# Centering ahead of the transposes and scaling by 1/std behind the projections, in the first segment of a fused attention and gMLP kernel

## The chip, the cores and the metric

The kernel runs on one core of a Trainium2 chip. Its time is the device time in microseconds (us) of one execution. A profiled execution also has a span, 1.7 to 1.8 us shorter than its time. Engines: TensorE (PE in the profile; PEld is its weight load), VectorE (DVE), ScalarE (ACT), GpSimd (POOL), SyncE (SP, which issues the DMAs here).

## The reference, cut to what matters

```python
def _layernorm(x, eps=1e-05):
    m = jnp.mean(x, axis=-1, keepdims=True)
    v = jnp.var(x, axis=-1, keepdims=True)
    return (x - m) / jnp.sqrt(v + eps)
# x: 2048 x 1024, handled in 4 segments of 512 rows; 32 heads of 32
# per segment: q, k, v = xn @ wq, xn @ wk, xn @ wv with xn = _layernorm(x),
# causal softmax attention within the segment, plus a memory of earlier segments
h  = x + A(_layernorm(x))        # attention, then @ wo
h2 = h + B(_layernorm(h))        # gMLP: two gelu halves, a 2048 x 2048 mixing, w_out
```

The change uses that a row's 1/std is one factor for that row: it may be applied to V's rows, and to the columns of transposed q and k, after the projections.

## The kernel before

The kernel records each operation on its engine's list, in program order, and derives waits from overlaps of memory cells of 32 bytes. TensorE and VectorE work their lists off in that order in the traces below (after the change, TensorE's ready V matmuls stand 2.69 us behind one that waits, and VectorE idles 1.53 us with statistics behind it whose chunk ScalarE had read from 4.33 us on). So the order of these lines is the order of work. The head of the kernel normalizes four chunks of 128 rows, transposes them on TensorE and projects V, k and q. Matrix products land in PSUM (ps in the traces), which this kernel lays out as eight banks; copying one out is called its eviction here. The gates are the sigmoid weights between attention and memory, the mask set-up spreads them into the table that the memory state is multiplied by, and phi is the function that the memory applies to q and k.

```python
warm(12)                        # dummy 128x512 matmuls
stats_of(0)                     # VectorE mean and variance, GpSimd 1/std
stats_of(1)
ln0 = ln_apply(XCH[0], ks[0])   # VectorE (x - mean) * rstd, bf16
pe_T(XNT[0], 0, ln0, (act, dve))  # 8 transposes, two copies out of PSUM
warm(3)
ln1 = ln_apply(XCH[1], ks[1])
stats_of(2)
pe_T(XNT[0], 1, ln1)
...                             # V quarters of 8 matmuls 128x256 between the chunks
proj_qk(0, 1); proj_qk(0, 0)    # k, then q, first 128 columns
v_quarter(3, 0); v_quarter(3, 1)
phi_exp(0); phi_max(0)
rot["banks"] = [6, 7]           # from here k, q, V and the memory state share two PSUM banks
# then per group of 4 heads: logits, k, pv, logits, state, q, logits, V ...
```

The eviction of q and k was one ScalarE copy from PSUM, in every segment:

```python
act.activation(QK[n % 2][:, which, :], bank(b), ACTF.Copy)
```

The softmax here doesn't subtract the row's maximum and nothing guards it: scores larger than these inputs give would overflow.

Of the kernel before, what the change touches and what calls it, by code (L numbers as in the profile page):

```python
# [5 lines left out]
BF16 = mybir.dt.bfloat16  # L6
F32 = mybir.dt.float32
I32 = mybir.dt.int32
ACTF = mybir.ActivationFunctionType
ALU = mybir.AluOpType  # L10

T = 2048
D = 1024
H = 32
NSEG = 4
L = 512
# [3 lines left out]
NQ = 8  # L20
# [237 lines left out]
def bass_sequential_preLN__memory_aug_infini_attn__mixer_gmlp__prompt_kernel(  # L258
# [17 lines left out]
    pe, act, dve, pool, sp = R.pe, R.act, R.dve, R.pool, R.sp  # L276

    K = 1024
# [4 lines left out]
    def tens(name, shape, dt, off):  # L283
        sz = int(np.prod(shape[1:])) * mybir.dt.size(dt)
        assert off % 32 == 0 and off + sz <= ARENA, (name, off, sz)
        t = nc.alloc_sbuf_tensor_at(name, list(shape), dt, offset=abase + off)
        R.space[t[:].tensor.name] = ("sbuf", off)
        return t
# [13 lines left out]
    cb = Bump(0, 14 * K)  # L302
    IDENT = cb("ident", [128, 128], BF16)
# [11 lines left out]
    MV = [cb("mv%d" % i, [128, 2], F32) for i in range(4)]  # L315
    RS = [cb("rs%d" % i, [128, 2], F32) for i in range(4)]
    RD = cb("rd", [128, 4, 4], F32)
    RDM = cb("rdm", [128, 4, 4], F32)


    HNT = [tens("hnT0", [128, 8, L], BF16, 14 * K), tens("hnT1", [128, 8, L], BF16, 22 * K),
           tens("hnT2", [128, 8, L], BF16, 30 * K), tens("hnT3", [128, 8, L], BF16, 38 * K)]
    XNT = [tens("xnT0", [128, 8, L], BF16, 30 * K), tens("xnT1", [128, 8, L], BF16, 38 * K)]
    WV = tens("wv", [128, 8, D], BF16, 46 * K)
    WQ = tens("wq", [128, 8, D], BF16, 62 * K)
    WK = tens("wk", [128, 8, D], BF16, 78 * K)
    WO = tens("wo", [128, 8, D], BF16, 94 * K)
    b1 = Bump(110 * K, 134 * K)
    XR = [b1("xr%d" % i, [128, D], BF16) for i in range(2)]
    HCH = [b1("hch%d" % i, [128, D], BF16) for i in range(3)]  # L330
    LNO = [b1("lno%d" % i, [128, D], BF16) for i in range(3)]
    OT = b1("oT", [128, NQ, L], BF16)
    b2 = Bump(134 * K, ARENA)
    XCH = [b2("xch%d" % i, [128, D], BF16) for i in range(4)]
    QK = [b2("qk%d" % i, [128, 2, L], BF16) for i in range(2)]
# [6 lines left out]
    V = b2("v", [128, 4, H, 34], BF16)  # L342
# [17 lines left out]
    PS = nc.alloc_psum_tensor("ps", [128, 8, 512], F32)  # L360
    R.space[PS[:, 0, :].tensor.name] = ("psum", 0)

    def bank(b):
        return PS[:, b, :]
# [6 lines left out]
    def next_bank():  # L371
        b = rot["banks"][rot["n"] % len(rot["banks"])]
        rot["n"] += 1
        return b

    def mm8(dst, lhs, rhs, n=8):
        for i in range(n):
            pe.matmul(dst, lhs(i), rhs(i), start=(i == 0), stop=(i == n - 1))


    def x_load(tc):
        sp.dma_start(XCH[tc % 4][:], x2d[tc * 128:(tc + 1) * 128, :])

    def wcols(ap, lo, hi):
        return ap[:, lo:hi].rearrange("(c p) n -> p c n", p=128)

    for tc in range(4):
        x_load(tc)
    sp.dma_start(WV[:, :, 0:256], wcols(A_wv, 0, 256))
    sp.dma_start(WV[:, :, 256:512], wcols(A_wv, 256, 512))  # L390
    sp.dma_start(WK[:, :, 0:256], wcols(A_wk, 0, 256))
    sp.dma_start(WQ[:, :, 0:256], wcols(A_wq, 0, 256))
    sp.dma_start(BETAB[:], A_beta.partition_broadcast(128))
    sp.dma_start(WV[:, :, 512:1024], wcols(A_wv, 512, D))


    pool.memset(MHALF[:], -0.5)
    dve.memset(ETMP[:], 0.0)
    act.activation(RDM[:, 0, 0:1], MHALF[:], ACTF.Exp)
    pool.iota(IOT[:], [[1, 128]], base=0, channel_multiplier=-1)  # L400
    pool.memset(V[:, :, :, 32:34], 1.0)
    pool.memset(BLK[:], 1.0)
    pool.affine_select(out=BLK[:], in_=BLK[:], pattern=[[-32, 4]], compare_op=ALU.is_ge, fill=0.0, base=0,
                       channel_multiplier=1)
    pool.affine_select(out=BLK[:], in_=BLK[:], pattern=[[32, 4]], compare_op=ALU.is_ge, fill=0.0, base=31,
# [3 lines left out]
    def gates():  # L409
        act.activation(GS[:], BETAB[:], ACTF.Exp, scale=-1.0)  # L410
        dve.tensor_single_scalar(GS[:], GS[:], 1.0, ALU.add)
        dve.reciprocal(GS[:], GS[:])
        dve.tensor_scalar(OMG[:].rearrange("p c i -> p (c i)"), GS[:], -1.0, 1.0, ALU.mult, ALU.add)
# [12 lines left out]
    def ln_stats(src):  # L426
        k = lnc[0] % 4
        lnc[0] += 1
        for i in range(2):
            dve.bn_stats(STATS[k][:, i, :], src[:, i * 512:(i + 1) * 512])  # L430
        dve.bn_aggr(MV[k][:], STATS[k][:])
        return k

    def ln_rstd(k):
        pool.tensor_single_scalar(RS[k][:, 0:1], MV[k][:, 1:2], float(LN_EPS), ALU.add)
        pool.tensor_tensor(RS[k][:, 1:2], RS[k][:, 0:1], MHALF[:], ALU.pow)
# [3 lines left out]
    def ln_apply(src, k):  # L440
        o = LNO[lno[0] % 3]
        lno[0] += 1
        dve.tensor_scalar(o[:], src[:], MV[k][:, 0:1], RS[k][:, 1:2], ALU.subtract, ALU.mult)
        return o

    def to_T(dst, tcl, src):
        sp.dma_start_transpose(dst[:, :, tcl * 128:(tcl + 1) * 128], src[:])

    def pe_T(dst, tcl, src, engines=(act,)):
        w = 8 // len(engines)  # L450
        for k, eng in enumerate(engines):
            bb = bank(next_bank()).bitcast(BF16)[:, 0:w * 128]
            for i in range(w):
                o = (k * w + i) * 128
                pe.transpose(bb[:, i * 128:(i + 1) * 128], src[:, o:o + 128], IDENT[:])
            d = dst[:, k * w:(k + 1) * w, tcl * 128:(tcl + 1) * 128]
            v = bb.rearrange("p (c n) -> p c n", c=w)
            if eng is act:
                act.activation(d, v, ACTF.Copy)
            else:  # L460
                dve.tensor_copy(d, v)


    def proj_v(s, tcl, half):
        proj_v_cols(s, tcl, half * 512, 512)

    def proj_v_cols(s, tcl, lo, w):
        b = next_bank()
        xt = XNT[s % 2]
        mm8(PS[:, b, 0:w], lambda i: xt[:, i, tcl * 128:(tcl + 1) * 128], lambda i: WV[:, i, lo:lo + w])  # L470
        act.activation(V[:, tcl, lo // 32:(lo + w) // 32, 0:32],
                       PS[:, b, 0:w].rearrange("p (h d) -> p h d", d=32), ACTF.Copy)

    def proj_qk(n, which):
        s, c = divmod(n, NQ)
        b = next_bank()
        xt = XNT[s % 2]
        w = WK if which else WQ
        mm8(bank(b), lambda i: w[:, i, c * 128:(c + 1) * 128], lambda i: xt[:, i, :])
        act.activation(QK[n % 2][:, which, :], bank(b), ACTF.Copy)  # L480

    def phi_views(n):
        s = n // NQ
# [4 lines left out]
    def phi_exp(n):  # L488
        q, p, e = phi_views(n)
        act.activation(e, q, ACTF.Exp)  # L490
# [47 lines left out]
    def mem_norm(n):  # L538
        om = PS[:, 0:4, 256:388].rearrange("p q (i d) -> p q i d", d=33)
        dve.tensor_single_scalar(RDM[:], om[:, :, :, 32], float(MEM_EPS), ALU.add)  # L540
        dve.reciprocal(RDM[:], RDM[:])
        dve.tensor_tensor(TM[n % 2][:], om[:, :, :, 0:32], RDM[:].unsqueeze(3).to_broadcast([128, 4, 4, 32]), ALU.mult)

    def norm(n):
# [10 lines left out]
        if c == NQ - 1:  # L555
            for tcl in range(4):
                to_T(OT, tcl, OTOK[s % 2][:, tcl, :])

# [19 lines left out]
    def wo(s, tcl, half):  # L578
# [3 lines left out]
        b = next_bank()  # L582
        mm8(bank(b), lambda i: OT[:, i, tcl * 128:(tcl + 1) * 128], lambda i: WO[:, i, half * 512:(half + 1) * 512])
        hs = slice(half * 512, (half + 1) * 512)
# [20 lines left out]
            lnq[1].append(it + (ln_stats(it[0]),))  # L605


    ks = {}

    def stats_of(tc):  # L610
        ks[tc] = ln_stats(XCH[tc])
        ln_rstd(ks[tc])

    def warm(k):
        for _ in range(k):
            pe.matmul(bank(7), IDENT[:], ETMP[:, 0, :], start=True, stop=True)

    def v_quarter(tcl, q):
        proj_v_cols(0, tcl, 256 * q, 256)

    warm(12)
    stats_of(0)
    stats_of(1)
    ln0 = ln_apply(XCH[0], ks[0])
    pe_T(XNT[0], 0, ln0, (act, dve))
    warm(3)
    ln1 = ln_apply(XCH[1], ks[1])
    stats_of(2)
    pe_T(XNT[0], 1, ln1)
    warm(2)  # L630
    stats_of(3)
    v_quarter(0, 0)
    v_quarter(0, 1)
    ln2 = ln_apply(XCH[2], ks[2])
    ln3 = ln_apply(XCH[3], ks[3])
    pe_T(XNT[0], 2, ln2)
    v_quarter(1, 0)
    v_quarter(1, 1)
    pe_T(XNT[0], 3, ln3)
    v_quarter(2, 0)  # L640
    v_quarter(2, 1)
    for tc in range(4, 8):
        x_load(tc)
    sp.dma_start(WK[:, :, 256:D], wcols(A_wk, 256, D))
    sp.dma_start(WQ[:, :, 256:D], wcols(A_wq, 256, D))
    gates()
    proj_qk(0, 1)
    proj_qk(0, 0)
    v_quarter(3, 0)
    v_quarter(3, 1)  # L650
    phi_exp(0)
    phi_max(0)
    rot["banks"] = [6, 7]
# [32 lines left out]
    for n in range(LAST + 1):  # L686
        s, c = divmod(n, NQ)
# [25 lines left out]
        def fill(lst):  # L713
            for u in lst:
                {"v": proj_v, "wo": wo, "qk": proj_qk, "z2": z2_group}[u[0]](*u[1:])
# [68 lines left out]
    for k in range(4, 8):  # L784
        lo, w = CH[k][1:]
        for fl in range(w // 128):
            fc = lo // 128 + fl
            for s in range(NSEG):
                b = next_bank()
# [11 lines left out]
    for tb in range(4):  # L801
        br = BROW[tb % 2]
# [3 lines left out]
        for fc in range(14):  # L806
            b = next_bank()
# [3 lines left out]
        for tcl in range(4):  # L811
            tc = 4 * tb + tcl
            fin = FIN[tc % 3]
            sp.dma_start(fin[:], out2d[tc * 128:(tc + 1) * 128, :])
            for lo, w in ((0, 512), (512, 512)) if tc < NTC - 1 else ((0, 512), (512, 256), (768, 256)):
                b = next_bank()
# [34 lines left out]
```

## Time and profile before

| | before |
|---|---|
| time, median (range) | 806.98 us (806.93 to 807.08, 4 runs) |
| TensorE busy | 796.1 of 805.2 us |
| first transposes start | 7.11 us |
| first V matmuls start | 9.59 us |
| first logits start | 21.91 us |
| first softmax tile ends | 24.68 us |

The busy table and the chain of work that ended last, from the page of the kernel before (busy us, share of the span, instructions; then shares of the chain):

```profile
span 805.2 us, 12550 instructions
...
PE 796.1 (99%) x5407; PEld 384.7 (48%) x5407; DVE 368.7 (46%) x756; ACT 301.8 (37%) x356; POOL 121.5 (15%) x234
...
PE 92%; DVE 5%; ACT 2%; issue 1%; DMA 0%
```

TensorE is the chain and it is full. What is gained or lost in the head, before it is full, goes straight into the time (after the change, the k of the sixth head group starts 4.15 us later and the span ends 4.0 later).

The timeline of TensorE before (start us, duration us, engine, line, operation, output and inputs, shapes, count, and in brackets the idle time ahead of it with what ended it):

```profile
7.11 0.62 PE L209 MATMUL ps<-ident,lno_88 128*128 128x128 bf16 x8 [0.43 <-DVE lno_88 L209]
...
9.59 1.04 PE L209 MATMUL ps<-wv,xnT_77 128*128 128x256 bf16 x8
...
16.61 1.89 PE L209 MATMUL ps<-xnT_77,wk 128*128 128x512 bf16 x8
18.34 1.89 PE L209 MATMUL ps<-xnT_77,wq 128*128 128x512 bf16 x8
20.06 1.91 PE L209 MATMUL ps<-wv,xnT_77 128*128 128x256 bf16 x16
21.91 0.39 PE L209 MATMUL ps<-qk_96 32*128 32x512 bf16 x4
...
24.73 0.40 PE L209 MATMUL ps<-qk_96 32*128 32x384 bf16 x8 [0.60 <-ACT e_104 L209]
```

A reader sees a short wait for VectorE's normalized chunk (lno; two like it are left out), then k, q and the last V back to back, then the logits, and at 24.73 the matmuls that waited for the first softmax tile (e). Eight matmuls of 512 columns take 1.73 us from start to start (16.61 to 18.34).

How one 1/std is made, from the timeline of VectorE and GpSimd before (same columns):

```profile
11.54 0.21 DVE L209 BATCH_NORM_AGGREGATE mv_66<-stats_62 128x2 f32<-128x12 f32 x1
...
11.83 0.40 POOL L209 TENSOR_SCALAR rs_70<-mv_66 128x1 f32<-128x1 f32 x1 [0.65 <-DVE mv_66 L209]
...
12.32 0.57 POOL L209 TENSOR_TENSOR rs_70<-rs_70,mhalf 128x1 f32<-128x1 f32 x1
...
12.92 0.55 DVE L209 TENSOR_SCALAR lno_88<-xch_95,mv_66,rs_70 128x1024 bf16<-128x1024 bf16 x1 [0.77 <-POOL rs_70 L209]
```

From the aggregate's end (11.75) to the first use of 1/std (12.92) pass 1.17 us. The statistics themselves take about 1.55 us a chunk.

### The profile page before, as it was taken

The numbers are of one execution on the slowest core, as the hardware profiler recorded it, in microseconds if no ns is written. First come the engines' busy times: TensorE is split into PE (matmuls) and PEld (weight loads), VectorE is DVE, ScalarE is ACT, GpSimd is POOL, SyncE is SP. The second block draws the span as 40 slices with busy tenths as digits, with TensorE's granted clock in tenths as the row PEclk, the third lists the DMA queues.
The fourth block names the chain that finished last, engine by engine and source line by source line (L and its number), as shares of the span: only waits on it lengthen the run. The fifth ranks groups of instructions, "written<-read, shape, count | busy, mean of one in ns | idle before, by whom it ended". The sixth has DMA issues, their size and how long they took to land.

```text
span 805.2 us, 12550 instructions
## 1 busy us (share of the span) xinstructions
PE 796.1 (99%) x5407; PEld 384.7 (48%) x5407; DVE 368.7 (46%) x756; ACT 301.8 (37%) x356; POOL 121.5 (15%) x234
## 2 busy tenths in 40 slices
PE   8999999999999999999999999999999999999998
PEld 4445544455444455455544444444444444444444
DVE  4653688669854585744463000054233324423332
ACT  3898876886778763233333333100000000000000
POOL 2342433233323231100131000000000000000000
PEclk9999999999999999999999999999999999999999
DMA  9782544455414057611115000550270044011002
GB/s 270 183 171 60 92 80 118 83 95 83 97 40 80 28 158 146 149 46 53 53 53 130 2 1 0 189 120 0 79 138 1 27 101 88 1 59 53 1 7 85
DMA packets 125992, 64.79 MB, mean 80 GB/s; under 512 B 94832, under 2 KB 114928, under 8 KB 125936
## 3 DMA queue, kind: packets, MB, share of 16 engines
q1 hardware_dynamic: 125936, 63.99, 34.1%
q8 instruction: 42, 0.69, 0.4%
q14 instruction: 14, 0.11, 0.1%
HBM read 32.51 MB, written 8.39 MB: 51 GB/s over the span
## 4 chain that ended last, share of the span: by engine, by line
PE 92%; DVE 5%; ACT 2%; issue 1%; DMA 0%
PE ps L209 92%; ACT e_105 L209 1%; DVE ta L209 1%; DVE stats_61 L209 0%; DVE stats_62 L209 0%; ACT e_108 L209 0%; DVE rdm L209 0%; DMA xch_92<-in_A_x_dram 0%; DVE hch_85 L209 0%; DVE rd L209 0%; ACT e_109 L209 0%; ACT e_106 L209 0%; DVE pqk_99 L209 0%; ACT e_104 L209 0%; DVE stats_59 L209 0%
## 5 line engine op out<-in xcount | busy, mean ns | idle before, releaser
L209 PE MATMUL ps<-w_out,yT 128*128 128x512 bf16 (+1 forms) x462 | 97.4, 373 | 0.0
L209 PE MATMUL ps<-wspT_121,z_119 128*128 128x512 bf16 x448 | 97.0, 379 | 0.0
L209 PE MATMUL ps<-wspT_122,z_119 128*128 128x512 bf16 x448 | 97.0, 379 | 0.0
L209 PEld LDWEIGHTS ps<-w_out,yT 128*128 128x128 bf16 x462 | 45.2, 98 | 51.7
L209 PEld LDWEIGHTS ps<-wspT_122,z_119 128*128 128x128 bf16 x448 | 43.8, 98 | 52.8
L209 PEld LDWEIGHTS ps<-wspT_121,z_119 128*128 128x128 bf16 x448 | 43.8, 98 | 52.9
L209 DVE TENSOR_TENSOR tmpg_128<-ps,brow_126 128x512 f32<-128x512 f32 x14 | 9.7, 691 | 117.1 <-DMA brow_126<-in_B_b_sp_dram 96.8
L209 ACT ACTIVATE z_119<-ps 128x448 bf16<-128x448 f32 x64 | 34.8, 544 | 75.1 <-PE ps L209 74.9
L209 PE MATMUL ps<-wo,oT 128*128 128x512 bf16 x256 | 58.4, 379 | 0.0
L209 ACT ACTIVATE z1T<-ps 128x512 bf16<-128x512 f32 x56 | 33.4, 597 | 63.3 <-PE ps L209 63.3
L209 DVE BATCH_NORM_STATS2 zst<-z_119 128x6 f32<-128x448 bf16 x64 | 39.1, 620 | 33.2 <-ACT z_119 L209 33.2
L209 PEld LDWEIGHTS ps<-wo,oT 128*128 128x128 bf16 x256 | 24.4, 98 | 27.4 <-issue 0.4
L209 ACT ACTIVATE e_107<-ps 128x2048 bf16<-128x2048 f32 x16 | 30.0, 1874 | 12.7 <-PE ps L209 12.7
L209 ACT ACTIVATE e_108<-ps 128x2048 bf16<-128x2048 f32 x16 | 30.0, 1877 | 10.7 <-PE ps L209 10.7
L209 ACT ACTIVATE e_104<-ps 128x2048 bf16<-128x2048 f32 x16 | 30.0, 1875 | 10.4 <-PE ps L209 10.4
L209 ACT ACTIVATE e_105<-ps 128x2048 bf16<-128x2048 f32 x16 | 30.0, 1877 | 9.8 <-PE ps L209 9.8
L209 PE MATMUL ps<-xnT_78,wk 128*128 128x512 bf16 x128 | 30.4, 380 | 0.0
L209 PE MATMUL ps<-xnT_77,wk 128*128 128x512 bf16 x128 | 30.4, 380 | 0.0
L209 PE MATMUL ps<-xnT_78,wq 128*128 128x512 bf16 x128 | 30.3, 379 | 0.0
L209 PE MATMUL ps<-xnT_77,wq 128*128 128x512 bf16 x128 | 30.2, 379 | 0.0
L209 PE MATMUL ps<-wv,xnT_77 128*128 128x512 bf16 (+1 forms) x160 | 29.9, 337 | 0.2 <-DMA wv<-in_A_wv_dram 0.2
L209 PE MATMUL ps<-wv,xnT_78 128*128 128x512 bf16 x128 | 29.6, 379 | 0.0
(218 smaller groups left out, 1171.6 us busy)
## 6 DMA issues: line engine op xcount, KB each, us to landing
w_out<-in_B_w_out_dram SPq DMA_DIRECT2D x1, 3584.0 KB, 12.7
wo<-in_A_wo_dram SPq DMA_DIRECT2D x1, 2048.0 KB, 9.9
xr_83<-in_A_x_dram SPq DMA_DIRECT2D x8, 256.0 KB, 3.3
xr_84<-in_A_x_dram SPq DMA_DIRECT2D x8, 256.0 KB, 3.9
win_116<-in_B_w_in_dram SPq DMA_DIRECT2D x2, 896.0 KB, 4.9
wk<-in_A_wk_dram SPq DMA_DIRECT2D x1, 1536.0 KB, 10.9
wq<-in_A_wq_dram SPq DMA_DIRECT2D x1, 1536.0 KB, 14.3
out_dram<-hch_85 SPq DMA_DIRECT2D x6, 256.0 KB, 3.0
```

Of the source, the lines that this page charges most:

```text
L209: ins = getattr(e, op.name)(*op.args, **op.kw)
```

## The change

It wants the transposes to start without waiting for 1/std. Chunks are only centered (chunks 1 to 3 with a mean from a ScalarE sum); 1/std is applied to V's rows in ScalarE's eviction, and to q's and k's columns by a VectorE product with a tile RB. RB is a broadcast of 1/std over the partitions, made by two matmuls of ones with diagonal tiles (a high and a low bf16 part). The first half of w_v comes in four pieces of 256 rows, so that V may start on the first piece. The core of the diff:

```diff
     def proj_qk(n, which):
...
-        act.activation(QK[n % 2][:, which, :], bank(b), ACTF.Copy)
+        qk_out(n, which, b)
+    def qk_out(n, which, b):
+        if n < NQ:                       # all 8 head groups of the first segment
+            dve.tensor_tensor(QK[n % 2][:, which, :], bank(b), RB[:], ALU.mult)
+        else:
+            act.activation(QK[n % 2][:, which, :], bank(b), ACTF.Copy)
+    MEAN = b1("mean", [128, 4], F32)     # 16 bytes: one 32-byte cell
+    def act_mean(tc):
+        act.activation(JUNK[:], XCH[tc][:], ACTF.Copy, scale=1.0 / D, accum_out=MEAN[:, tc:tc + 1])
+    def rstd0(tc, k):
+        ln_rstd(k)
+        pool.tensor_copy(RS0[:, tc:tc + 1], RS[k][:, 1:2])
+        dve.tensor_single_scalar(DIAG[0][:, tc, :], IDENT[:], RS[k][:, 1:2], ALU.mult)
+        dve.scalar_tensor_tensor(DIAG[1][:, tc, :], IDENT[:], RS[k][:, 1:2], DIAG[0][:, tc, :], ALU.mult, ALU.subtract)
     warm(12)
+    act_mean(1)
+    k0 = ln_stats(XCH[0])
+    c0 = center(0, MV[k0][:, 0:1])
+    c1 = center(1, MEAN[:, 1:2])
+    pe_Th(0, c0, dve, dve)
+    act_mean(2)
+    pe_Th(1, c1, act, dve)
+    act_mean(3)
+    c2 = center(2, MEAN[:, 2:3])
+    warm(2)
+    vb = [next_bank() for _ in range(2)]
+    for i in range(6):
+        for t in range(2):
+            v_mm(0, t, 0, vb[t], i)
+    pe_Th(2, c2, act, dve)
+    rstd0(0, k0)
+    c3 = center(3, MEAN[:, 3:4])
+    k1 = ln_stats(XCH[1])
+    ...                                  # the last 4 of these V matmuls
+    pe_Th(3, c3, act, dve)
+    v_out(0, 0, 0, vb[0])
+    k2 = ln_stats(XCH[2])
+    rstd0(1, k1)
+    v_out(0, 1, 0, vb[1])
+    k3 = ln_stats(XCH[3])
+    rstd0(2, k2)
+    proj_v(0, 2, 0)
+    rstd0(3, k3)
+    mm8(bank(bk), lambda i: WK[:, i, 0:128], lambda i: XNT[0][:, i, :])
+    for i in range(2):
+        pe.matmul(bank(br), ONES[:], DIAG[i][:].rearrange("p c n -> p (c n)"), start=(i == 0), stop=(i == 1))
+    act.activation(RB[:], bank(br), ACTF.Copy)
+    qk_out(0, 1, bk)
+    mm8(bank(bq), lambda i: WQ[:, i, 0:128], lambda i: XNT[0][:, i, :])
+    qk_out(0, 0, bq)
+    proj_v(0, 3, 0)
...
     gates()
-    proj_qk(0, 1)
-    proj_qk(0, 0)
-    v_quarter(3, 0)
-    v_quarter(3, 1)
     phi_exp(0)
```

More of the change, by code (lines that the diff above doesn't have):

```diff
@@ L318, in bass_sequential_preLN__memory_aug_infini_attn__mixer_gmlp__prompt_kernel @@
     RDM = cb("rdm", [128, 4, 4], F32)
+    RS0 = cb("rs0", [128, 4], F32)
     HNT = [tens("hnT0", [128, 8, L], BF16, 14 * K), tens("hnT1", [128, 8, L], BF16, 22 * K),
@@ L323, in bass_sequential_preLN__memory_aug_infini_attn__mixer_gmlp__prompt_kernel @@
     XNT = [tens("xnT0", [128, 8, L], BF16, 30 * K), tens("xnT1", [128, 8, L], BF16, 38 * K)]
-    WV = tens("wv", [128, 8, D], BF16, 46 * K)
+    WV = [tens("wv%d" % i, [128, 8, 512], BF16, (46 + 8 * i) * K) for i in range(2)]
     WQ = tens("wq", [128, 8, D], BF16, 62 * K)
@@ L332, in bass_sequential_preLN__memory_aug_infini_attn__mixer_gmlp__prompt_kernel @@
     OT = b1("oT", [128, NQ, L], BF16)
+    b1 = Bump(110 * K, 120 * K)
+    ONES = b1("ones", [128, 128], BF16)
+    MEAN = b1("mean", [128, 4], F32)
+    RB = b1("rb", [128, L], F32)
+    DIAG = [b1("diag%d" % i, [128, 4, 128], BF16) for i in range(2)]
+    JUNK = b1("junk", [128, D], BF16)
     b2 = Bump(134 * K, ARENA)
@@ L388, in bass_sequential_preLN__memory_aug_infini_attn__mixer_gmlp__prompt_kernel @@
         x_load(tc)
-    sp.dma_start(WV[:, :, 0:256], wcols(A_wv, 0, 256))
-    sp.dma_start(WV[:, :, 256:512], wcols(A_wv, 256, 512))
+    for i in range(0, 8, 2):
+        sp.dma_start(WV[0][:, i:i + 2, :],
+                     A_wv[i * 128:(i + 2) * 128, 0:512].rearrange("(c p) n -> p c n", p=128))
     sp.dma_start(WK[:, :, 0:256], wcols(A_wk, 0, 256))
@@ L393, in bass_sequential_preLN__memory_aug_infini_attn__mixer_gmlp__prompt_kernel @@
     sp.dma_start(BETAB[:], A_beta.partition_broadcast(128))
-    sp.dma_start(WV[:, :, 512:1024], wcols(A_wv, 512, D))
+    sp.dma_start(WV[1][:], wcols(A_wv, 512, D))
     pool.memset(MHALF[:], -0.5)
@@ L402, in bass_sequential_preLN__memory_aug_infini_attn__mixer_gmlp__prompt_kernel @@
     pool.memset(BLK[:], 1.0)
+    pool.memset(ONES[:], 1.0)
     pool.affine_select(out=BLK[:], in_=BLK[:], pattern=[[-32, 4]], compare_op=ALU.is_ge, fill=0.0, base=0,
@@ L461, in pe_T, with v_out, v_mm @@
                 dve.tensor_copy(d, v)
+    def v_out(s, tcl, half, b):
+        act.activation(V[:, tcl, 16 * half:16 * half + 16, 0:32], bank(b).rearrange("p (h d) -> p h d", d=32),
+                       ACTF.Copy, scale=RS0[:, tcl:tcl + 1] if s == 0 else 1.0)
+    def v_mm(s, tcl, half, b, i):
+        pe.matmul(bank(b), XNT[s % 2][:, i, tcl * 128:(tcl + 1) * 128], WV[half][:, i, :],
+                  start=(i == 0), stop=(i == 7))
     def proj_v(s, tcl, half):
-        proj_v_cols(s, tcl, half * 512, 512)
-    def proj_v_cols(s, tcl, lo, w):
         b = next_bank()
-        xt = XNT[s % 2]
-        mm8(PS[:, b, 0:w], lambda i: xt[:, i, tcl * 128:(tcl + 1) * 128], lambda i: WV[:, i, lo:lo + w])
-        act.activation(V[:, tcl, lo // 32:(lo + w) // 32, 0:32],
-                       PS[:, b, 0:w].rearrange("p (h d) -> p h d", d=32), ACTF.Copy)
+        for i in range(8):
+            v_mm(s, tcl, half, b, i)
+        v_out(s, tcl, half, b)
     def proj_qk(n, which):
@@ L605, in bg_pop @@
             lnq[1].append(it + (ln_stats(it[0]),))
-    ks = {}
-    def stats_of(tc):
-        ks[tc] = ln_stats(XCH[tc])
-        ln_rstd(ks[tc])
     def warm(k):
@@ L616, in warm @@
             pe.matmul(bank(7), IDENT[:], ETMP[:, 0, :], start=True, stop=True)
-    def v_quarter(tcl, q):
-        proj_v_cols(0, tcl, 256 * q, 256)
-    warm(12)
-    stats_of(0)
-    stats_of(1)
-    ln0 = ln_apply(XCH[0], ks[0])
-    pe_T(XNT[0], 0, ln0, (act, dve))
-    warm(3)
-    ln1 = ln_apply(XCH[1], ks[1])
-    stats_of(2)
-    pe_T(XNT[0], 1, ln1)
-    warm(2)
-    stats_of(3)
-    v_quarter(0, 0)
-    v_quarter(0, 1)
-    ln2 = ln_apply(XCH[2], ks[2])
-    ln3 = ln_apply(XCH[3], ks[3])
@@ L636, in bass_sequential_preLN__memory_aug_infini_attn__mixer_gmlp__prompt_kernel, with center @@
-    pe_T(XNT[0], 2, ln2)
-    v_quarter(1, 0)
-    v_quarter(1, 1)
-    pe_T(XNT[0], 3, ln3)
-    v_quarter(2, 0)
-    v_quarter(2, 1)
+    def center(tc, mean):
+        o = LNO[tc % 3]
+        dve.tensor_single_scalar(o[:], XCH[tc][:], mean, ALU.subtract)
+        return o
+    def act_mean(tc):
[5 more added lines that the diff above has]
+        dve.scalar_tensor_tensor(DIAG[1][:, tc, :], IDENT[:], RS[k][:, 1:2], DIAG[0][:, tc, :], ALU.mult, ALU.subtract)
@@ new lines, in pe_Th @@
+    def pe_Th(tcl, src, e0, e1):
+        pe_T(XNT[0], tcl, src, (e0, e1))
+    warm(12)
+    act_mean(1)
[7 more added lines that the diff above has]
+    c2 = center(2, MEAN[:, 2:3])
+    warm(2)
+    vb = [next_bank() for _ in range(2)]
[3 more added lines that the diff above has]
+    pe_Th(2, c2, act, dve)
@@ new lines, in bass_sequential_preLN__memory_aug_infini_attn__mixer_gmlp__prompt_kernel @@
+    rstd0(0, k0)
+    c3 = center(3, MEAN[:, 3:4])
+    k1 = ln_stats(XCH[1])
+    for i in range(6, 8):
+        for t in range(2):
+            v_mm(0, t, 0, vb[t], i)
+    pe_Th(3, c3, act, dve)
[7 more added lines that the diff above has]
+    rstd0(3, k3)
+    bk, bq, br = next_bank(), next_bank(), next_bank()
+    mm8(bank(bk), lambda i: WK[:, i, 0:128], lambda i: XNT[0][:, i, :])
```

## The prediction

> **What bounds it now.** TensorE is busy 99% of the 805.2 us span (busy table), and the table of waits has it idle for only about 6 us in all. From 27 us on the chain of waits is almost TensorE alone. So only the first 27 us can give time, and what is gained or lost there passes one for one to the end. In the timeline, TensorE's warm-up matmuls run until 6.7, the first transposes start at 7.11, V at 9.6, k at 16.6, q at 18.3, the last V piece at 20.06, the first logits at 21.9; then ScalarE decides (V copy, exp, first softmax tile, ends 24.68). To 12.2 the chain is VectorE: statistics (1.55 us a chunk), 1/std, apply, four times.
>
> **What the change does.** It takes 1/std from ahead of the transposes. Means of chunks 1 to 3 come from ScalarE (about 1.05 us a chunk, from its 128x1024 activations). But the first transposes can gain only 0.4 us: the 12 warm-up matmuls (0.42 us each) hold TensorE until 6.7. One 32-byte cell holds all four means, and the recorded waits order whole cells: the second mean waits for the centering of chunk 1, the centering of chunk 2 for the mean of chunk 3. The third chunk's transposes now stand behind 12 V matmuls (0.216 us each, 2.6 us).
>
> k and q now need the row of 1/std, and that needs all four statistics. VectorE does these late: it waits until about 11.6 for the third chunk's transposes, and only then do the copy (0.42), two diagonals (0.35), centering (0.45), statistics 1 (1.55), copy (0.45), statistics 2 (1.55), diagonals, statistics 3 (1.55), GpSimd's rstd (1.17 from aggregate to use, as at 11.75 to 12.92) and the last diagonals follow. Sum: the broadcast matmuls start at about 20.0. TensorE has finished k at about 17 and, in order, cannot start q; it idles about 3 us. Then broadcast 0.43, q 1.73, V 1.73: logits at about 24 instead of 21.9. The V copy, gates and exp on ScalarE stand between, so the first softmax tile ends about 2.5 us later.
>
> Second loss: all 16 k,q evictions of segment 0 go from ScalarE (0.60) to VectorE (estimate 0.69, as its 128x512 f32 addition from PSUM). ScalarE's relief is worth little: TensorE is full there (idle 0.8 us between 22 and 90). On VectorE the mask set-up (4.15 us) now comes after the second q; behind it and the phi step stands the third k's eviction, whose bank the third q needs: TensorE waits about 1.3 us, perhaps 0.4 once more. After that VectorE (5 of 8 us busy, plus 1.4) keeps up. Later segments: unchanged.
>
> Weights: row pieces of 1 KB lines should land no later than the two halves (second at 10.7 us); I expect no long wait for them.
>
> **Predicted: 810.8 us, 80% range 808.5 to 813.5.** Faster by over 2%: 0.005; within 2%: 0.985; slower by over 2%: 0.01.
>
> **Right if:** first V matmuls about 1 us earlier, but an idle TensorE of 2 to 3.5 us before the broadcast matmuls, put down to VectorE's diagonals; first logits near 24; another wait of about 1 us at the third q, for VectorE; the same spacing from 45 us on.
>
> **Wrong if:** VectorE is sooner done with the statistics (weights landing early and shorter copies): then nearly nothing changes. [...]

The figure of 810.8 us is the sum of 807.0 for the kernel before, about 2.5 for the later first softmax tile and about 1.3 for the third q. Of the durations, 0.35 us for two diagonals and 0.69 for an eviction by VectorE are estimates; the trace after the change shows 0.50 to 0.55 and 0.69.

## The result, and the profile after

The changed kernel took 811.0 us in the median (809.21 to 811.52, 4 runs) against 806.98 us. The ratio of the runs is 1.0046, 95% interval 1.0028 to 1.0063: slower by about 0.5%, which counts as the same at a limit of 2%. (Ratios are the mean time of one kernel's runs over that of the other's of the same rounds, so not quite the ratio of the medians.) The four times fall in two groups: 809.21 us, with a mean granted TensorE clock of 1.000, and 810.93, 811.08 and 811.52 us, with 0.998. The profiled run is that of 810.93 us.

The page after, the lines that answer to those of before:

```profile
span 809.2 us, 12521 instructions
...
PE 797.3 (99%) x5374; PEld 382.0 (47%) x5374; DVE 383.3 (47%) x784; ACT 295.8 (37%) x342; POOL 122.8 (15%) x239
...
PE 94%; DVE 3%; ACT 2%; issue 0%; POOL 0%; ACTq 0%
```

The span grew by 4.0 us. TensorE's waits in the first 90 us after (who waited for whom: us in total, times, longest):

```profile
PE ps L209 <- DVE diag_97 L209: 2.7, 1, 2.7
...
PE ps L209 <- ACT e_112 L209: 1.1, 1, 1.1
...
PE ps L209 <- DVE qk_104 L209: 0.3, 1, 0.3
```

The first and the third of these are new, the second was 0.6 us before (left out: the wait at the start of the program, one of 0.6 us for the centering of the fourth chunk and one of 0.2 us for the second softmax tile). Above all, TensorE stood 2.7 us before the broadcast matmuls, for the last diagonal. TensorE's timeline after shows what came of it:

```profile
6.49 0.61 PE L209 MATMUL ps<-ident,lno_90 128*128 128x128 bf16 x8
...
7.81 2.75 PE L209 MATMUL ps<-wv_80,xnT_78 128*128 128x512 bf16 x12
...
12.93 1.89 PE L209 MATMUL ps<-wv_80,xnT_78 128*128 128x512 bf16 x8
14.66 1.89 PE L209 MATMUL ps<-xnT_78,wk 128*128 128x512 bf16 x8
19.24 0.39 PE L209 MATMUL ps<-diag_97,ones 128*128 128x512 bf16 x1 [2.69 <-DVE diag_97 L209]
...
19.92 3.51 PE L209 MATMUL ps<-xnT_78,wq 128*128 128x512 bf16 x8
23.27 1.89 PE L209 MATMUL ps<-wv_80,xnT_78 128*128 128x512 bf16 x8
25.09 0.40 PE L209 MATMUL ps<-qk_104 32*128 32x512 bf16 x4
```

V starts 1.78 us earlier than before (7.81 against 9.59) and k 1.95 us earlier (14.66 against 16.61). Then TensorE idles from about 16.5 to 19.24, and q takes 3.35 us from start to start (19.92 to 23.27) instead of 1.73. The logits start at 25.09, 3.18 us later than before. The granted clock explains q; stretches of one us after (window, length, then busy us and instructions of PE, PEld, DVE, ACT and POOL, granted clock, DMA share, GB/s):

```profile
17.00:18.00 1.00, 0.00 (x0) 0.00 (x0) 0.96 (x3) 0.69 (x1) 0.06 (x1) 1.00 0.57 197
...
19.00:20.00 1.00, 0.76 (x3) 0.29 (x4) 0.53 (x2) 0.00 (x0) 0.20 (x1) 0.88 0.82 281
20.00:21.00 1.00, 1.00 (x4) 0.38 (x3) 0.21 (x1) 0.60 (x1) 0.00 (x0) 0.50 0.90 283
...
23.00:24.00 1.00, 1.00 (x6) 0.44 (x5) 0.53 (x1) 0.00 (x0) 0.00 (x0) 0.91 1.05 379
```

The clock halved for 3.41 us: stretches of 0.1 us put its fall at 19.77 and its return at 23.18. (This column does not show the slow start of the kernel: it reads 1.00 between 3 and 7 us too, where the loads of the warm-up matmuls follow each other every 0.43 us at first.) Why VectorE was late is in its own timeline after:

```profile
9.03 0.49 DVE L209 TENSOR_SCALAR lno_92<-xch_102,mean 128x1024 bf16<-128x1024 bf16 x1 [1.02 <-ACT junk L209]
11.05 0.42 DVE L209 COPY xnT_78<-ps 128x512 bf16<-128x512 bf16 x1 [1.53 <-PE ps L209]
...
12.33 1.42 DVE L209 BATCH_NORM_STATS2 stats_60<-xch_101 128x6 f32<-128x512 bf16 x2
...
16.27 1.41 DVE L209 BATCH_NORM_STATS2 stats_62<-xch_103 128x6 f32<-128x512 bf16 x2
...
18.93 0.25 DVE L209 TENSOR_SCALAR diag_97<-ident,rs_70 128x128 bf16<-128x128 bf16 x1 [0.49 <-POOL rs_70 L209]
```

VectorE idled 1.02 us for the mean of chunk 3 and 1.53 us for the third chunk's transposes; only after that did it do three of the four statistics, which then end at 17.94. (On ScalarE each mean took 1.04 to 1.06 us, and a separate read of its accumulator after it 0.18 to 0.19.) The last 1/std is there at 18.9. Later on, the k projection of the sixth head group starts at 52.31 us before and at 56.46 after, 7.60 and 7.61 us behind that of the fifth. The loss is complete by then.

### The profile page after: what moved, and what is told of

The parts are those of the page before. It is cut to its first block, busy times and chain, and to the rows that moved or that the text cites. A ratio compares the mean times of both kernels' runs of the same rounds, so it can differ in the third digit from the quotient of the medians.

```text
span 809.2 us, 12521 instructions
## 1 busy us (share of the span) xinstructions
PE 797.3 (99%) x5374; PEld 382.0 (47%) x5374; DVE 383.3 (47%) x784; ACT 295.8 (37%) x342; POOL 122.8 (15%) x239
## 3 DMA queue, kind: packets, MB, share of 16 engines
HBM read 32.51 MB, written 8.39 MB: 51 GB/s over the span
## 4 chain that ended last, share of the span: by engine, by line
PE 94%; DVE 3%; ACT 2%; issue 0%; POOL 0%; ACTq 0%
PE ps L209 94%; ACT e_116 L209 0%; ACT e_113 L209 0%; DVE maskg L209 0%; ACT e_117 L209 0%; ACT e_114 L209 0%; DVE rdm L209 0%; ACT e_112 L209 0%; DVE ta L209 0%; DVE tm_120 L209 0%; DVE stats_62 L209 0%; DVE stats_60 L209 0%; DVE stats_61 L209 0%; DVE hch_87 L209 0%; DVE pqk_107 L209 0%
## 5 line engine op out<-in xcount | busy, mean ns | idle before, releaser
L209 ACT ACTIVATE e_113<-ps 128x2048 bf16<-128x2048 f32 x16 | 30.0, 1877 | 11.6 <-PE ps L209 11.6
L209 PE MATMUL ps<-xnT_78,wq 128*128 128x512 bf16 x128 | 31.9, 394 | 0.3 <-DVE qk_104 L209 0.3
L209 PE MATMUL ps<-xnT_79,wq 128*128 128x512 bf16 x128 | 30.3, 379 | 0.0
L209 POOL TENSOR_SCALAR_AFFINE_SELECT e_113<-e_113 128x512 bf16<-128x512 bf16 x32 | 21.2, 685 | 34.6 <-ACT e_113 L209 34.6
L209 POOL TENSOR_SCALAR_AFFINE_SELECT e_116<-e_116 128x512 bf16<-128x512 bf16 x32 | 20.2, 655 | 38.1 <-ACT e_116 L209 38.1
```

The costliest lines, as they stand in the source:

```text
L209: ins = getattr(e, op.name)(*op.args, **op.kw)
```

## The experiments

Ten experiments, each with five rounds; all gave correct results. The kernel before took 806.9, 807.09 and 806.93 us in the three sessions.

### The changed kernel again

No edit.

> The changed kernel unaltered. Theory: its time has two values, about 811 us where the TensorE clock halves during the wait for the broadcast matmuls (mean granted clock 0.998) and about 809.3 where it does not (1.000); the wait itself (2.7 us) is there in every run. Rival (the spread is chance of DMA or of the whole chip): times spread without a tie to the clock value.

Measured: 809.09, 810.71, 811.79, 811.83 and 809.19 us. The two runs at 809.1 and 809.2 have clock 1.000, the other three 0.998. The profiled run is one that kept its clock:

```profile
19.08 0.78 PE L209 MATMUL ps<-diag,ones 128*128 128x512 bf16 x2 [2.69 <-DVE diag L209]
19.69 1.89 PE L209 MATMUL ps<-xnT,wq 128*128 128x512 bf16 x8
21.42 1.89 PE L209 MATMUL ps<-wv,xnT 128*128 128x512 bf16 x8
23.24 0.39 PE L209 MATMUL ps<-qk 32*128 32x512 bf16 x4
...
26.55 0.40 PE L209 MATMUL ps<-qk 32*128 32x384 bf16 x8 [1.08 <-ACT e L209]
```

The wait of 2.69 us is the same, q takes 1.73 us, and the logits start at 23.24. So the halved clock comes on top of the wait, in some runs. By estimate, 3.41 us at half the rate (granted clock 0.50) lose 1.7 us of TensorE work.

### Dummy matmuls in the wait

```diff
     mm8(bank(bk), lambda i: WK[:, i, 0:128], lambda i: XNT[0][:, i, :])
+    warm(12)
     for i in range(2):
         pe.matmul(bank(br), ONES[:], ...)
```

> The changed kernel with 12 dummy 128x512 matmuls (about 2.6 us) between the k projection and the broadcast matmuls, so the wait stays but TensorE is not idle in it. Theory (about 1.6 us of the 4 are a halved clock that the idle stretch brought on): every run near 809.3, clock 1.000, q projection 1.73 us from start to start instead of 3.35. Rival (the halving has nothing to do with the idle stretch, or is made up for later): 811 as before, or slower by the dummies.

Measured: 809.33 us (809.08 to 809.78), clock 1.000 in all five runs. The broadcast matmuls still start at 19.12 us and q takes 1.73 us. So the idle stretch brings on the halving here: six of the nine runs of the changed kernel had it, none of these five, in which TensorE was kept at work (busy for 2.90 of the 3 us from 17 to 20). 2.4 us of loss remain (809.33 less 806.9).

### The fourth V ahead of the broadcast

```diff
     mm8(bank(bk), ...)
+    for i in range(8):
+        v_mm(0, 3, 0, b3, i)
     for i in range(2):
         pe.matmul(bank(br), ONES[:], ...)
     act.activation(RB[:], bank(br), ACTF.Copy)
+    v_out(0, 3, 0, b3)
...
     qk_out(0, 0, bq)
-    proj_v(0, 3, 0)
```

> The changed kernel with the V projection of the fourth chunk moved ahead of the broadcast matmuls. Theory (TensorE stands in order behind work that VectorE holds up): V fills 1.7 us of the 2.7 us wait, about 1 us of idle is left, the clock stays whole, the first logits wait for the q eviction and start near 22.3 instead of 25.1; total 807.2 to 808.0. Rival A (VectorE evictions of k and q in the first segment cost the 4 us): about 811 as before. Rival B (only the clock counts): about 809.3.

Measured: 807.51 us (807.36 to 808.08), clock 1.000 in all runs. TensorE in this run:

```profile
16.88 1.89 PE L209 MATMUL ps<-wv,xnT 128*128 128x512 bf16 x8
19.73 0.78 PE L209 MATMUL ps<-diag,ones 128*128 128x512 bf16 x2 [0.96 <-DVE diag L209]
20.34 1.89 PE L209 MATMUL ps<-xnT,wq 128*128 128x512 bf16 x8
23.02 0.40 PE L209 MATMUL ps<-qk 32*128 32x512 bf16 x4 [0.79 <-DVE qk L209]
```

V fills the wait down to 0.96 us, and a wait of 0.79 us for the eviction of q appears in front of the logits, which V had hidden. The logits start 0.7 us later than expected, in a profiled run that is the slowest of the five (808.08) and began V late (8.30 us, against 7.81 in the changed kernel); the median lies within the stretch expected. Moving eight matmuls takes 3.2 us off the median of the changed kernel: 1.6 of clock and about 1.6 of waiting.

### The kernel before with k and q evicted by VectorE

```diff
-        act.activation(QK[n % 2][:, which, :], bank(b), ACTF.Copy)
+        if n < NQ:
+            dve.tensor_tensor(QK[n % 2][:, which, :], bank(b), RB[:], ALU.mult)   # RB: a tile of ones
+        else:
+            act.activation(QK[n % 2][:, which, :], bank(b), ACTF.Copy)
```

> The kernel before with the 16 k and q evictions of the first segment moved from ScalarE to VectorE, as a product with a tile of ones of the same shape as the broadcast 1/std; everything else as before. Theory (the evictions are the small part): 807.0 to 808.3, with at most one wait of TensorE for the third k eviction. Rival (the evictions carry the loss): 810 or more.

Measured: 807.37 us (807.26 to 807.42), so 0.47 us slower than before; the ratio's interval (0.9992 to 1.0019) holds 1 and allows a loss of up to 1.5 us. The waits of TensorE in its first 90 us hold the one foreseen:

```profile
PE ps L209 <- DVE qk L209: 0.3, 1, 0.3
```

The evictions are the smaller part of the loss of 4.0 us.

### Statistics of chunk 1 earlier

```diff
     act_mean(3)
+    k1 = ln_stats(XCH[1])
     c2 = center(2, MEAN[:, 2:3])
...
     c3 = center(3, MEAN[:, 3:4])
-    k1 = ln_stats(XCH[1])
```

> The changed kernel with the statistics of chunk 1 (1.55 us) moved ahead of the centering of chunk 2, into the stretch in which VectorE waits. Theory (the wait of TensorE is set by the row of VectorE work between the third chunk's transposes and the last diagonal): the broadcast matmuls come about 1.5 us earlier, the wait falls from 2.7 to about 1.2, the clock stays whole in all runs, total about 807.7. Rival (the wait is set by GpSimd's rstd or by when the chunks or weights land): the wait stays at 2.7 and the times at 809 to 812.

Measured: 810.4 us (809.09 to 810.45); 0.998 in three runs, 1.000 in two. This expectation failed, and so did its rival's number for the wait. The waits of TensorE and of VectorE in this run:

```profile
PE ps L209 <- DVE diag L209: 2.0, 1, 2.0
```
```profile
11.54 0.42 DVE L209 COPY xnT<-ps 128x512 bf16<-128x512 bf16 x1 [1.12 <-PE ps L209]
...
12.43 0.48 DVE L209 TENSOR_SCALAR lno<-xch,mean 128x1024 bf16<-128x1024 bf16 x1
13.63 0.42 DVE L209 COPY xnT<-ps 128x512 bf16<-128x512 bf16 x1 [0.71 <-PE ps L209]
```

The wait fell by 0.7 us only, to 2.0. VectorE now comes to the copy of chunk 3 before the transposes are done, which themselves wait for the centering that stands just ahead on VectorE (12.43), so it idles a new 0.71 us. Filling one gap opened another: from the copy of chunk 2 to the last diagonal VectorE takes 7.16 us (11.54 to 18.70) where it took 7.88 in the profiled rerun (10.88 to 18.76). In this run V also started later (8.30 against 7.54), because TensorE's matmuls turned fast later (their loads still came every 0.43 us up to 6.69 us, in the rerun up to 4.70; the twelve warm-up matmuls took 5.30 us against 4.23), so the broadcast matmuls start at 19.01, hardly sooner than the 19.08 of the rerun. The median moved by 0.3 us and the lowest time not at all.

### Own cells for the means

```diff
-    MEAN = b1("mean", [128, 4], F32)
+    MEAN = b1("mean", [128, 4, 8], F32)      # and MEAN[:, tc, 0:1] in its uses
```

> The changed kernel with a 32-byte cell for each mean, so the second mean no longer waits for the centering of chunk 1. Theory (the transposes of chunk 2 stand behind 12 V matmuls anyway): chunk 2 is centered about 1 us earlier, TensorE starts V at most 0.3 us earlier, time unchanged: 809.0 without and 811 with the halved clock. Rival (the false waits on means cost time): 808 or less without the halved clock.

Measured: 808.86 and 809.93 us at clock 1.000, 811.66 to 811.82 at 0.998. Chunk 2 is centered at 7.59 in place of 9.03 us, and nothing is gained: its transposes still stand behind twelve V matmuls. In the profiled run (809.93 us) these waited for the first piece of w_v and started at 8.39 us, so V came no earlier in it:

```profile
PE ps L209 <- DVE diag L209: 2.7, 1, 2.7
...
PE ps L209 <- DMA wv<-in_A_wv_dram: 0.8, 1, 0.8
```

The false wait on the means is real and costs nothing as long as the V matmuls stand in front.

### The kernel before with row pieces of w_v

```diff
-    sp.dma_start(WV[:, :, 0:256], wcols(A_wv, 0, 256))
-    sp.dma_start(WV[:, :, 256:512], wcols(A_wv, 256, 512))
+    for i in range(0, 8, 2):
+        sp.dma_start(WV[:, i:i + 2, 0:512],
+                     A_wv[i * 128:(i + 2) * 128, 0:512].rearrange("(c p) n -> p c n", p=128))
```

> The kernel before with the first half of w_v loaded as four row pieces in place of two column halves, nothing else changed. Theory (the pieces are not where time goes): all of it lands by about 9.5 to 10 us; the first V quarter waits some tenths of a us, the second no longer does; 806.5 to 807.3. Rival (the pieces delay the start): 808 or more.

Measured: 806.94 us (806.83 to 807.15) against 807.09. In this run no V matmul waits for w_v, not even in the first quarter, where some tenths were expected; before, the second quarter did (0.20 us). The pieces neither cost nor bring anything here.

### VectorE's order mended

```diff
     act_mean(3)
+    k1 = ln_stats(XCH[1])
     c2 = center(2, MEAN[:, 2:3])
...
-    pe_Th(2, c2, act, dve)
     rstd0(0, k0)
     c3 = center(3, MEAN[:, 3:4])
-    k1 = ln_stats(XCH[1])
+    pe_Th(2, c2, act, dve)
...
+    k2 = ln_stats(XCH[2])
     pe_Th(3, c3, act, dve)
     v_out(0, 0, 0, vb[0])
-    k2 = ln_stats(XCH[2])
```

> The changed kernel with only VectorE's order mended: statistics of chunk 1 before the centering of chunk 2, diagonals and centering of chunk 3 before the copies of chunk 2, statistics of chunk 2 before the copies of chunk 3; TensorE's order as in the change. Theory (the order of VectorE's work set the wait): the broadcast matmuls come about 2 us earlier, near 17, the wait falls to about 1[...], first logits near 21.2, total 806.7 to 807.5 in all runs. Rival (TensorE's order is what counts, as the run with the fourth V first suggests): 808.5 or more, with the halved clock in some runs.

Measured: 807.26 us (806.8 to 807.59), clock 1.000 in all runs, as in the five of the fourth V first, where the profiled wait was 0.96 us. TensorE's timeline:

```profile
14.34 1.89 PE L209 MATMUL ps<-xnT,wk 128*128 128x512 bf16 x8
17.22 0.78 PE L209 MATMUL ps<-diag,ones 128*128 128x512 bf16 x2 [0.99 <-DVE diag L209]
...
21.39 0.40 PE L209 MATMUL ps<-qk 32*128 32x512 bf16 x4
...
24.70 0.40 PE L209 MATMUL ps<-qk 32*128 32x384 bf16 x8 [1.08 <-ACT e L209]
```

The broadcast matmuls start at 17.22 instead of 19.24, the wait is 0.99 us, and the logits start half a us earlier than in the kernel before. Yet the time is that of before (ratio 1.0002, 0.999 to 1.0015): ScalarE still has V, gates and exp to do ahead of the first softmax tile, which ends at 24.64, as before at 24.68, and TensorE then waits for VectorE at the third q. (The trace says 0.54 us there, but it holds only seven of the eight matmuls of q; with the missing one put in, the wait is about 0.3.) This is the single most telling run: the operations are those of the change, in another order on VectorE alone.

### Both orders mended, and the softmax tile freed

On top of the previous edit (with own cells for the means) the fourth V goes ahead of the broadcast, and the gates and the mask set-up move into gaps:

```diff
     rstd0(2, k2)
     proj_v(0, 2, 0)
+    mask_blk()                 # 8 small mask copies, in the wait for the last 1/std
     rstd0(3, k3)
     mm8(bank(bk), ...)         # k
+    for i in range(8):
+        v_mm(0, 3, 0, b3, i)
     ...                        # broadcast, RB
     qk_out(0, 1, bk)
+    gates()
+    v_out(0, 3, 0, b3)
     mm8(bank(bq), ...)         # q
     qk_out(0, 0, bq)
-    proj_v(0, 3, 0)
...
-    gates()
     phi_exp(0)
     phi_max(0)
+    mask_gs(True)              # half of the rest; the other half where mask_g() was
```

> The changed kernel reordered: statistics of chunk 1 before the centering of chunk 2, diagonals and centering of chunk 3 before the copies of chunk 2, fourth V ahead of the broadcast, gates and the mask set-up spread over gaps of VectorE, own cells for the means. Theory: no wait of TensorE above 0.6 us after the first transposes, first logits near 20.8, first softmax tile ends near 23.1 instead of 24.7 before, total 805.2 to 806.2, faster than both kernels. Rival (the idea of centered transposes cannot gain, VectorE work being the floor): 807 or more.

Measured: 805.21 us (804.74 to 805.59), ratio 0.9976 (0.9964 to 0.9989) to the kernel before: faster than both kernels, if only by 0.2% than the kernel before. What each of the moves is worth was not measured apart. The one wait of TensorE above 0.2 us in the first 90 us, after that at the start:

```profile
PE ps L209 <- DVE qk L209: 1.0, 1, 1.0
```

The logits start at 20.92 us and the first softmax tile ends at 23.25, both about as expected. One wait missed the limit of 0.6 us: 0.97 us for the eviction of q.

### The fourth V in two halves

```diff
-    for i in range(8):
+    for i in range(4):
         v_mm(0, 3, 0, b3, i)
...
-    v_out(0, 3, 0, b3)
     mm8(bank(bq), ...)         # q
+    for i in range(4, 8):
+        v_mm(0, 3, 0, b3, i)
     qk_out(0, 0, bq)
...
     phi_max(0)
+    dve.tensor_single_scalar(V[:, 3, 0:16, 0:32], ..., RS0[:, 3:4], ALU.mult)
```

> The best version so far with the fourth V cut in two halves of four matmuls, one ahead of the broadcast and one behind q, and its eviction on VectorE. Theory (what is left are the waits for the diagonals and for the q eviction, about 1 us in all, and half a V hides each): first logits near 20.4 instead of 20.9, total 804.4 to 805.0. Rival (the added VectorE work gives it back): 805.2 or more.

Measured: 804.9 us (804.7 to 805.34), ratio 0.9975 (0.9961 to 0.9988).

```profile
20.41 0.40 PE L209 MATMUL ps<-qk 32*128 32x512 bf16 x4
```

The logits start at 20.41 us and no wait above 0.2 us is left between 8 and 90 us. The gain over the previous version cannot be told from the spread of both: against the kernel before in its own session, this version is 2.0 us faster and the previous one 1.9.

## Why the prediction was right

The range held 811.0 us, and the direction and the main mechanism were right. Point by point:

- *The first transposes gain only 0.4 us, for the warm-up matmuls hold TensorE.* The profiled run after started them 0.62 us earlier (6.49 against 7.11). In two other profiled runs the warm-up matmuls turned fast earlier (near 4.7 us in both, here near 6), and the transposes started at 5.80 (the rerun) and 5.63 (the dummy matmuls). In the profiled run V came 1.78 us earlier where about 1 was forecast.
- *VectorE makes the four 1/std late, and TensorE idles about 3 us in front of the broadcast.* Shown: 2.69 us, put down to the last diagonal. The steps of VectorE came out as listed, but for a pair of diagonals (0.50 to 0.55 us from start to start); the start of the copy of chunk 2 was at 11.05 instead of 11.6, and most of the difference between 19.24 and 20.0 for the broadcast comes from that. The run with VectorE's order mended shows the cause: the broadcast comes 2.0 us earlier and the loss is gone. TensorE's order is the other half of it: in the trace the V matmuls that were ready stood 2.69 us behind the broadcast, and moving them ahead took the wait to 0.96 us.
- *Logits near 24.* 25.09 us in the run with the halved clock, 23.24 in the one without.
- *A second loss of 1.3 to 1.7 us by the k and q evictions on VectorE.* Right in kind, mis-sized: TensorE's wait at the third q was 0.31 us, the second wait ("perhaps 0.4") did not come, and the evictions alone, put into the kernel before, cost 0.47 us, which is not clear of noise. One term of the sum was too large and accounts for 0.7 of the 1 us: the mask set-up took 3.45 us (31.28 to 34.73) where 4.15 were taken from the kernel before, because its eight small copies took 0.67 us instead of 1.50. Before, two of the eight were long, one until 28.42 and one until 29.25, and GpSimd's masking of the softmax tiles ended at 28.40 and 29.23; after, GpSimd was idle meanwhile. With both orders mended and with V in halves the eight copies took 0.68 us, again with no masking beside them. Whether the masking made the two copies long, no run tested.
- *The clock, which is no term of the sum.* It fell in three of the four runs of the result and three of five of the rerun, and cost 1.6 us at q (3.35 us from start to start instead of 1.73). So the middle of the range, 810.8 us, was met by luck, through errors that cancel: about 1 us too much for the third q, about 0.7 too much for the first softmax tile (2.5 us later was forecast; in the rerun that kept its clock TensorE got past it at 26.55 us, where it was 24.73 before, so 1.8), and 1.6 us of clock left out. Without the fall the kernel takes 809.1 to 809.2 us, still within the range.
- *Weights no later than before.* Right: the row pieces alone change nothing, although V, which now starts sooner, waited up to 0.75 us for the first piece in some runs.
- *The false wait on the means.* Seen (ScalarE waited 0.85 us for the centering of chunk 1), without effect on the time.

As a sum for the profiled run: k starts 1.95 us earlier, the wait takes 2.69, the broadcast 0.68 (19.24 to 19.92) and the halved clock 1.6, which makes 3.0 of the 3.18 us by which the logits come later; then the softmax tile comes 3.67 later, the third q (37.03 against 32.90) 4.13, and the span ends 4.0 later. Of this 1.6 is clock, and most of the rest comes from the wait.

What stays open is why the clock falls in some executions only. The runs of the three kernels with a profiled wait of 2.0 to 2.7 us (the changed kernel in both sessions, the earlier statistics, the own cells) show a mean clock of 0.998 in 12 of 19, and those of the four kernels whose longest wait in the head after the warm-up was 1.1 us or less (the fourth V first, VectorE's order mended, both orders mended, the fourth V in halves) in none of 20. One of the twelve has a trace: in it the clock fell at 19.77 us, 0.53 us after the first broadcast matmul had started behind 2.69 us of idle, and stayed at 0.50 for 3.41 us. The rerun's trace has the same wait of 2.69 us and no fall. What decides between the two was not shown.

## What to carry to other kernels

Taking a factor out of the front of a chain moves its deadline, it does not remove the work: look at who needs it next (here q, through the broadcast) and place the engine's work for that deadline into the gaps that the change opens. A ready group of matmuls should not be recorded behind one that waits for another engine: moving one ahead took the wait here from 2.69 to 0.96 us. Half of the group on each side hid two waits in the trace, with a gain in time too small to measure. An idle stretch of TensorE of 2.69 us cost another 1.6 us of clock here, in some runs only, so two groups of times in a repeated run are worth a look at the granted clock of each.
